# Decoding one f tile's weights ahead of the token forms, and storing the forms from other buffers

## The chip, the cores and the metric

The program runs on one core of a Trainium2 chip. The metric is the device time of one execution in microseconds, the median of several runs. The profile is of one further execution of the same program.

## The reference

Band attention (4 batches, 8 heads, 512 local and 32 global tokens, head size 64) gives 2176 tokens of 512 numbers. Two MLPs of the same size follow; each has 512 inputs, 2048 hidden units and 512 outputs:

```python
x = attention_out                      # 2176 x 512
h = x @ w_in                           # 512 -> 2048
g = np.where(h > 0, h, np.exp(np.minimum(h, 0)) - 1)
x = g @ w_out                          # 2048 -> 512
h = x @ w_in2
g = np.where(h >= 1, h, np.where(h <= -1, 0, (h + 1) ** 2 / 4))
out = g @ w_out2
```

Weights come as 64-bit floats and everything is done to more than single precision of one product: each factor is split into a high and a low part, and a product is three matmuls (low·high, high·low, high·high).

## The kernel before, in words

**Tiles.** The hidden units are cut into 16 f tiles of 128. Local tokens are cut into four blocks j of 512; the 128 global rows are a fifth block. `xh[j]`, `xl[j]` are the high and low parts of a token block, in two halves of [128, 2, 512]. An up product of one f tile and one block is 12 matmuls (L281), followed by the curve on ScalarE (L301, L303), the join on VectorE (L313), and the split into `gh` (ScalarE, L330) and `gl` (VectorE, L334). A down product is 12 matmuls into four PSUM banks (L368); at the end of a group of f tiles each bank goes through `collect`: ScalarE copies it to a tile `ev` (L347; four buffers), and a DMA stores it to DRAM (group of f tiles 0 to 2, from the SP queue, L350) or adds it there (later groups, an accumulating DMA from the GpSimd queue, L352).

**Stages of the first MLP.** `PLAIN = [[0, 1, 2], [3]]`: f tiles 0 to 3 are computed with plain products, 0 to 2 with weights that were decoded during the attention, f tile 3 with weights decoded behind it. f tiles 4 to 15, and the whole second MLP, are computed by pairs of f tiles with a Strassen-like scheme (`quad`, L1053): it needs seven "forms" of each duo of token blocks (X11, X21, X22 are halves of the blocks themselves; T2, T3, T1, T4 are sums and differences of them), each again in a high and a low part.

**Forms.** `first_forms(duo)` makes them for the first MLP: GpSimd adds high and low parts of four halves (L861: two into a tile `sum` of the pool `wraw`, two into the single buffers `top` and `rest`), VectorE makes four differences, and each of T2, T3, T1, T4 is split (`split`: ScalarE L951, VectorE L861) into a tile `form` and stored to DRAM (`keep`, two DMAs of 512 KB, L958). X11, X21 and X22 are stored from where they are. Before the first pair, T2, T3, T1 and T4 of duo 0 are loaded back (`load_form`, L1026) into the places of token blocks 2 and 3, once these have been used with f tile 3.

**Weights.** `words` loads raw 64-bit words (1 MB, L867) into a tile `wraw`; `decode` turns them into a high and a low part with two instructions on ScalarE (L213, L237) and seven on VectorE (L216 to L239), through the single buffers `top` and `rest`. `decode_one` does f tile 3 (into a tile tagged `wo0`). `decode_in(n)` does the first layer's side of pair n into a tile tagged `wi0`, `wi1` or `wi2` ([128, 2, 2048], 16 KB a partition), and then makes the Strassen sums of the weights on GpSimd (`whole`, `mixed`, L861), ScalarE (L909) and GpSimd again (`wi`). `decode_out(n)` does the second layer's side.

**Buffers.** The pool `wraw` has two buffers of 8 KB a partition. In the kernel before raw words, the tile `sum` and each tile `form` all go through it, in program order (`in_order("wraw", ...)`).

**Order.** The code issues work by events. An event is one up product or one part of a quad; after it one waiting group of down products is issued, and one or two background jobs go one step further. `job_at(n, job)` starts a job behind event n. Events 0 to 6 are the remaining up products of f tiles 0 to 2, event 7 the global rows, and then come the four up products of f tile 3. A scheduler then lays out each engine's queue: it follows that order, but puts an instruction that its model of times finds ready ahead of one that is not. On the chip each engine works its queue strictly in order.

Of the kernel before, what the change touches and what calls it, by code (L numbers as in the profile page):

```python
# [11 lines left out]
F32R = mybir.dt.float32r  # L12
# [9 lines left out]
B, H, SL, SG, D = 4, 8, 512, 32, 64  # L22
# [4 lines left out]
P = 128  # L27
# [13 lines left out]
PLAIN = [[0, 1, 2], [3]]  # L41
# [28 lines left out]
X11, X21, T2, T1, T3, T4, X22 = range(7)  # L70
# [7 lines left out]
def band_attention_then_two_mlps(  # L78
# [35 lines left out]
    def token_tile(j, h, part):  # L114

        return plain_p.tile([P, 2, SL], F32R, tag=f"x{part}{j}{h}", name="x" + "hl"[part])
# [59 lines left out]
    def in_order(tag, ins):  # L176


        if eng is free:
            if tag in newest:  # L180
                tc.add_manual_dep(ins.ins, newest[tag].ins.name, IN_ORDER, reason="order of tiles")
            newest[tag] = ins
# [241 lines left out]
    def mpool(name, bufs, **kw):  # L424
        return ctx.enter_context(tc.tile_pool(name=name, bufs=bufs, reuse_waits="tile", **kw))
# [424 lines left out]
    wraw_p = mpool("wraw", 2, side="right")  # L850
    wtmp_p = mpool("wtmp", 1, side="right")
    w_ps = [mpool("w_more", 1, side="right")]
# [6 lines left out]
    def add(out, a, b, op=ALU.add, engine=None):  # L859

        return (engine or eng.vector).tensor_tensor(out, a, b, op)  # L861

    def words(n, srcs):

        raw = wraw_p.tile([P, n * len(srcs)], U64, tag="wraw", name="wraw")
        for i, src in enumerate(srcs):
            ins = eng.sync.dma_start(raw[:, i * n:(i + 1) * n], src)  # L867
            if i == 0:
                in_order("wraw", ins)
        return raw  # L870

    def decode_one(f):

        w = w_ps[0].tile([P, 2, WCOLS], F32R, tag="wo0", name="wo")
        raw = words(WCOLS, [w1[f]])
        yield
        for _ in decode(wtmp_p, raw, w[:, 0], w[:, 1]):
            pass
        rows_in[0, 1] = lambda k, part: w[:, part, k * P:(k + 1) * P].rearrange("p (f c) -> p f c", f=1)
        w_in[0, f] = [w[:, i, 0:KT * P] for i in range(2)]  # L880
        w_out[0, f] = [w[:, i, KT * P:] for i in range(2)]

    def of_pair(n):

        layer, q = (0, n + 2) if n < 6 else (1, n - 6)
        return layer, (2 * q, 2 * q + 1)

    def decode_in(n):

        layer, fs = of_pair(n)  # L890
        raw = words(KT * P, [(w1, w2)[layer][f][:, 0:KT * P] for f in fs])
        yield
        w = w_ps[n % 3 // 2].tile([P, 2, 8 * BLOCK], F32R, tag=f"wi{n % 3}", name="wi")
        for _ in decode(wtmp_p, raw, w[:, 0, 0:4 * BLOCK], w[:, 1, 0:4 * BLOCK]):
            pass
        yield
        x = wtmp_p.tile([P, 4 * BLOCK], F32, tag="rest", name="whole")
        y = wtmp_p.tile([P, 4 * BLOCK], F32, tag="top", name="mixed")
        at = lambda t, c: t[:, c % (4 * BLOCK):c % (4 * BLOCK) + BLOCK]
        whole = add(  # L900
            x, w[:, 0, 0:4 * BLOCK].bitcast(F32), w[:, 1, 0:4 * BLOCK].bitcast(F32), engine=eng.gpsimd
        )
        in_order("rest", whole)
        in_order("top", add(at(y, S1), at(x, A21), at(x, A22), engine=eng.gpsimd))
        add(at(y, S2), at(y, S1), at(x, A11), ALU.subtract, eng.gpsimd)
        add(at(y, S3), at(x, A11), at(x, A21), ALU.subtract, eng.gpsimd)
        add(at(y, S4), at(x, A12), at(y, S2), ALU.subtract, eng.gpsimd)
        hi = w[:, 0, 4 * BLOCK:]
        eng.scalar.activation(hi, y, AF.Copy)  # L909
        add(w[:, 1, 4 * BLOCK:], y, hi.bitcast(F32), ALU.subtract, eng.gpsimd)  # L910
        pairs_in[n] = w
        rows_in[1, n] = lambda k, part: w[:, part, 0:4 * BLOCK].rearrange("p (f c) -> p f c", f=2)[
            :, :, k * P:(k + 1) * P
        ]

    def decode_out(n):

        layer, fs = of_pair(n)
        i = (n + 1) % 3
        raw = words(DM, [(w1, w2)[layer][f][:, KT * P:] for f in fs])  # L920
        yield

        while w_out_uses.get(n - 3):
            yield
        while len(w_ps) < 2:
            yield
        if i < 2:
            w = w_ps[i].tile([P, 2, 2, DM], F32R, tag=f"wo{i}", name="wo")
            w = [w[:, part] for part in range(2)]
        else:  # L930
            w = [token_tile(1, 0, part) for part in range(2)]
        for _ in decode(wtmp_p, raw, *(part.rearrange("p f d -> p (f d)") for part in w)):
            pass
        for i, f in enumerate(fs):
            w_out[layer, f] = [part[:, i] for part in w]
# [4 lines left out]
    def flat(t):  # L940

        return t.rearrange("p k n -> p (k n)")
# [6 lines left out]
    def split(out, src):  # L949

        ins = eng.scalar.activation(out[0], src, AF.Copy)  # L951
        add(out[1], src, out[0].bitcast(F32), ALU.subtract)
        return ins

    def keep(form, key, after=None):

        for part in range(2):
            ins = eng.sync.dma_start(forms[key][:, part], form[part].bitcast(F32))  # L958
            if after is not None:
                tc.add_manual_dep(ins.ins, after.ins.name, LANDED, reason="behind the loads")  # L960
        made_forms.add(key)

    def first_forms(duo):

        j0, j1 = 2 * duo, 2 * duo + 1
        s = wraw_p.tile([P, 2, 2 * SL], F32, tag="wraw", name="sum")
        x11, x21 = s[:, 0], s[:, 1]
        x12, x22 = (wtmp_p.tile([P, 2 * SL], F32, tag=tag, name="half") for tag in ("top", "rest"))
        for out, j, h, tag in ((x11, j0, 0, "wraw"), (x12, j1, 0, "top"), (x22, j1, 1, "rest"), (x21, j0, 1, "")):
            high, low = (flat(x[j][h]).bitcast(F32) for x in (xh, xl))  # L970
            ins = add(out, high, low, engine=eng.gpsimd)
            if tag:
                in_order(tag, ins)
        for i, j, h in ((X11, j0, 0), (X21, j0, 1), (X22, j1, 1)):
            keep([flat(x[j][h]) for x in (xh, xl)], (0, duo, i), last_low[0])
        yield
        add(x11, x12, x11, ALU.subtract)
        add(x12, x22, x12, ALU.subtract)
        add(x22, x22, x11, ALU.subtract)
        add(x21, x21, x22, ALU.subtract)  # L980
        for i, src in ((T2, x22), (T3, x12), (T1, x11), (T4, x21)):
            t = wraw_p.tile([P, 2, 2 * SL], F32R, tag="wraw", name="form")
            t = [t[:, part] for part in range(2)]
            in_order("wraw", split(t, src))
            keep(t, (0, duo, i))
            if i == T3:
                yield

    def later_forms(duo):
# [219 lines left out]
    def job_at(n, job, ahead=True):  # L1209

        due.setdefault(n, []).append((job, ahead))

    job_at(0, first_forms(0), False)
    job_at(2, first_forms(1), False)
    job_at(4, decode_one(PLAIN[1][0]))
    job_at(7, decode_in(0))
    job_at(9, decode_out(0))
    job_at(11, decode_in(1))
    for i, js in enumerate(((0, 1, 2, 3), (2, 3, 0, 1))):
        fs = PLAIN[i]  # L1220
        for j in js:
# [131 lines left out]
```

## Time and profile before

| | |
|---|---|
| runs | 891.52, 893.14, 897.77 us; median 893.14 us |
| profiled execution | 890.76 us, of which the span of the trace 889.0 us |
| mean granted TensorE clock | 0.975 of full speed |
| busy in the span | PE 818.1 us, VectorE 687.3 us, ScalarE 553.0 us, GpSimd 247.3 us |

PE is the matmul array, DVE VectorE, ACT ScalarE, POOL GpSimd, SP the SyncE queue that issues most DMAs. "L951" is line 951 of the kernel. Bracketed text behind an instruction is the idle time of its engine just before it, and what ended it. A DMA share is the mean busy share of the core's 16 DMA engines in a stretch; it can come out a little over 1.

### The profile page before, as it was taken

The page shows a single profiled execution, that of the slowest core. Times are in us where ns is not written, and L with a number is a line of the kernel's source. Part 1 is how long each engine was busy: PE and PEld are TensorE (multiplying, and loading weights), DVE is VectorE, ACT ScalarE, POOL GpSimd, SP SyncE. Part 2 cuts the span into 40 slices and gives each one's busy share as a digit, 9 for nine tenths or more (in the row PEclk, how much of TensorE's full clock was granted, in tenths as well). Part 3 has the DMA queues.
Part 4 walks back from the last instruction along what each step waited for, and adds up shares of the span by engine and source line. Part 5 has one row for each costly group of instructions (what it writes and reads, how often), then busy time and mean ns, then how long its engine had stood idle before and what let it go on. Part 6 is the DMA issues. An engine that isn't in the chain of part 4 may idle for free.

```text
span 889.0 us, 15955 instructions
## 1 busy us (share of the span) xinstructions
PE 818.1 (92%) x6058; PEld 663.3 (75%) x6058; DVE 687.3 (77%) x1187; ACT 553.0 (62%) x948; POOL 247.3 (28%) x254
## 2 busy tenths in 40 slices
PE   7899999906969999999999996999989999999998
PEld 5677778705757888888888875787878888888886
DVE  5888865518839799888797989999998699765464
ACT  5788846515636557665555537777776786777461
POOL 2222242203460724633240020214235143511000
PEclk9999999957989999999999999999999999999999
DMA  8978719577997738962972874725685398339723
GB/s 272 326 245 283 225 40 398 216 258 259 221 218 284 132 106 215 306 152 43 263 253 93 314 255 167 262 94 189 225 232 112 70 308 234 52 74 282 260 94 107
DMA packets 67132, 180.88 MB, mean 203 GB/s; under 512 B 9328, under 2 KB 9584, under 8 KB 65904
## 3 DMA queue, kind: packets, MB, share of 16 engines
q1 hardware_dynamic: 55248, 158.62, 51.1%
q0 software_dynamic: 11520, 20.98, 15.6%
q8 instruction: 48, 0.79, 0.4%
q10 hardware_dynamic: 288, 0.26, 0.1%
q14 instruction: 28, 0.23, 0.1%
HBM read 116.65 MB, written 63.18 MB: 202 GB/s over the span
## 4 chain that ended last, share of the span: by engine, by line
PE 54%; DVE 20%; issue 7%; ACT 6%; DMA 6%; POOL 6%; SPq 0%; ACTq 0%; POOLq 0%; DVEq 0%
PE dn L368 24%; PE up L1053 18%; DVE u L861 3%; DVE gl L334 2%; DVE g L315 2%; DMA sum<-ev 2%; PE up L281 2%; POOL mixed L861 2%; DVE rest L220 2%; POOL whole L861 2%; PE s L146 2%; PE dn L381 2%; DVE top L233 1%; POOL sum L352 1%; DMA wraw<-in_w 1%
## 5 line engine op out<-in xcount | busy, mean ns | idle before, releaser
L1053 PE MATMUL up<-xh,wi 128*128 128x512 f32 x784 | 263.2, 395 | 8.9 <-DVE u L861 6.0
L368 PE MATMUL dn<-gh,wo 128*128 128x512 f32 x608 | 189.3, 394 | 8.6 <-ACT ev L347 5.2
L1053 PEld LDWEIGHTS up<-xh,wi 128*128 128x128 f32 x784 | 148.7, 190 | 44.2 <-DVE u L861 9.4
L861 DVE TENSOR_TENSOR u<-up,u 128x512 f32<-128x512 f32 x196 | 130.6, 682 | 44.3 <-PE up L1053 26.5
L1053 PE MATMUL up<-xl,wi 128*128 128x512 f32 x392 | 154.2, 393 | 0.0
L368 PEld LDWEIGHTS dn<-gh,wo 128*128 128x128 f32 x608 | 113.1, 189 | 35.9 <-ACT ev L347 9.3
L330 ACT ACTIVATE gh<-g 128x512 fp32r<-128x512 f32 x123 | 77.2, 630 | 71.9 <-DVE g L315 35.4
L352 POOL DMA_DIRECT2D sum<-ev x80 | 75.3, 1167 | 160.9 <-ACT ev L347 160.0
L334 DVE TENSOR_TENSOR gl<-g,gh 128x512 fp32r<-128x512 f32 x123 | 101.8, 832 | 20.1 <-ACT gh L330 18.8
L368 PE MATMUL dn<-gl,wo 128*128 128x512 f32 x304 | 116.8, 391 | 0.3 <-DVE gl L334 0.3
L861 POOL TENSOR_TENSOR whole<-wi 128x1024 f32<-128x1024 f32 x14 | 36.7, 2619 | 257.8 <-DVE wi L239 246.7
L1053 PEld LDWEIGHTS up<-xl,wi 128*128 128x128 f32 x392 | 74.5, 190 | 15.1
L347 ACT ACTIVATE ev<-dn 128x512 f32<-128x512 f32 x110 | 61.3, 593 | 32.9 <-DMA sum<-ev 23.7
L315 DVE TENSOR_TENSOR g<-u,g 128x512 f32<-128x512 f32 x64 | 59.9, 940 | 27.8 <-ACT g L308 27.8
L306 ACT ACTIVATE g<-u,half_sb 128x512 f32<-128x512 f32 x64 | 46.0, 721 | 46.6 <-DVE u L861 40.0
L368 PEld LDWEIGHTS dn<-gl,wo 128*128 128x128 f32 x304 | 57.3, 189 | 12.9 <-DVE gl L334 0.7
L368 PE MATMUL dn<-gh,xl 128*128 128x512 f32 x160 | 62.5, 393 | 0.5 <-DVE xl L239 0.4
L368 PE MATMUL dn<-gh,xh 128*128 128x512 f32 x160 | 62.3, 390 | 0.0
L368 PE MATMUL dn<-gl,xh 128*128 128x512 f32 x160 | 59.2, 389 | 0.0
L301 ACT ACTIVATE g<-u 128x512 f32<-128x512 f32 x48 | 30.0, 627 | 42.3 <-DVE u L861 36.8
L307 ACT ACTIVATE g<-g,one_sb 128x512 f32<-128x512 f32 x68 | 48.6, 719 | 1.3
L313 DVE SCALAR_TENSOR_TENSOR g<-u,g 128x512 f32<-128x512 f32 x48 | 38.3, 803 | 13.3 <-ACT g L303 13.3
(189 smaller groups left out, 1488.5 us busy)
## 6 DMA issues: line engine op xcount, KB each, us to landing
wraw<-in_w SPq DMA_DIRECT2D x56, 512.0 KB, 6.1
xl<-form SPq DMA_DIRECT2D x46, 512.0 KB, 7.4
xh<-form SPq DMA_DIRECT2D x46, 512.0 KB, 9.0
sum<-ev POOLq DMA_DIRECT2D x80, 256.0 KB, 7.7
v_sb<-in_vwin SPq DMA_DIRECT2D x64, 260.0 KB, 4.9
form<-xh SPq DMA_DIRECT2D x20, 512.0 KB, 3.8
form<-xl SPq DMA_DIRECT2D x20, 512.0 KB, 4.0
sum<-ev SPq DMA_DIRECT2D x32, 256.0 KB, 3.1
```

Source lines behind the costliest of these rows:

```text
L301: eng.scalar.activation(self.g, self.ps, AF.Exp)
L306: eng.scalar.activation(self.g, self.ps, AF.Relu, bias=half_sb, scale=-0.5)
L307: eng.scalar.activation(self.g, self.g, AF.Relu, bias=one_sb, scale=-1.0)
L313: eng.vector.scalar_tensor_tensor(g, self.ps, 0.0, g, ALU.max, ALU.subtract)
L315: eng.vector.tensor_tensor(g, self.ps, g, ALU.max)
L330: eng.scalar.activation(self.gh, self.g, AF.Copy)
L334: eng.vector.tensor_tensor(self.gl, self.g, self.gh.bitcast(F32), ALU.subtract)
L347: eng.scalar.activation(out, ps, AF.Copy)
L352: eng.gpsimd.dma_start(to, out, accum_op=ALU.add)
L368: eng.tensor.matmul(banks[d], w[:, d * P:(d + 1) * P], g, start=first and k == 0, stop=last and k == 2)
L861: return (engine or eng.vector).tensor_tensor(out, a, b, op)
L1053: eng.tensor.matmul(ps, w[:, a, col + k * P:col + (k + 1) * P], x[b][:, k * SL:(k + 1) * SL], start=k + t == 0, stop=k == 1 and t == 2,)
```

## The change

Two things. The jobs start in another order: `decode_one` of f tile 3 at event 0, the forms of duo 0 at event 1 and of duo 1 at event 3 (before: forms at 0 and 2, `decode_one` at 4), and the first three jobs on pairs one or two events earlier. And the eight tiles `form` no longer come from the pool `wraw`: T2 and T3 of a duo go into one tile tagged `wi0`, T1 and T4 into one tile tagged `wi1`, the two single buffers that pairs 0 and 1 take later for their weights.

```diff
-        for i, src in ((T2, x22), (T3, x12), (T1, x11), (T4, x21)):
-            t = wraw_p.tile([P, 2, 2 * SL], F32R, tag="wraw", name="form")
-            t = [t[:, part] for part in range(2)]
-            in_order("wraw", split(t, src))
-            keep(t, (0, duo, i))
-            if i == T3:
+        for i, pair in enumerate((((T2, x22), (T3, x12)), ((T1, x11), (T4, x21)))):
+
+            t = w_ps[0].tile([P, 2, 2, 2 * SL], F32R, tag=f"wi{i}", name="form")
+            for k, (form, src) in enumerate(pair):
+                split([t[:, k, part] for part in range(2)], src)
+                keep([t[:, k, part] for part in range(2)], (0, duo, form))
+            if i == 0:
                 yield
...
-    job_at(0, first_forms(0), False)
-    job_at(2, first_forms(1), False)
-    job_at(4, decode_one(PLAIN[1][0]))
-    job_at(7, decode_in(0))
-    job_at(9, decode_out(0))
-    job_at(11, decode_in(1))
+    job_at(0, decode_one(PLAIN[1][0]))
+    job_at(1, first_forms(0), False)
+    job_at(3, first_forms(1), False)
+    job_at(5, decode_in(0))
+    job_at(8, decode_out(0))
+    job_at(10, decode_in(1))
```

## Rows read from the trace of the kernel before

**Rows 1.** The page, the span in 40 slices of 22.2 us: busy tenths, and granted TensorE clock.
```profile
PE   7899999906969999999999996999989999999998
PEclk9999999957989999999999999999999999999999
```
**Rows 2.** Waits of PE from 100 us on: waiter, releaser, total us, times, longest.
```profile
PE up L281 <- DVE wo L239: 30.6, 1, 30.6
PE up L1053 <- DVE u L861: 6.0, 5, 2.4
PE dn L368 <- ACT ev L347: 5.2, 5, 3.0
```
**Rows 3.** Chain of waits, 176 to 207 us: start, us, what.
```profile
181.34 1.06 ACT form L951
182.43 1.24 DVE form L861
183.68 2.64 DMA form<-form
186.42 1.06 ACT form L951
...
193.84 0.32 SPq L958
...
194.26 5.89 DMA wraw<-in_w
...
200.17 0.70 DVE rest L216
...
205.48 1.24 DVE wo L239
```
**Rows 4.** Timeline of PE around that wait: start, us, instruction.
```profile
175.81 0.39 PE L368 MATMUL dn<-gl,wh 128*128 128x512 f32 x1
206.76 0.79 PE L281 MATMUL up<-xh,wo 128*128 128x512 f32 x1 [30.56 <-DVE wo L239]
212.47 0.55 PE L281 MATMUL up<-xl,wo 128*128 128x512 f32 x1
226.72 0.40 PE L1053 MATMUL up<-xh,wi 128*128 128x512 f32 x1
```
**Rows 5.** Stretches of the span: length, busy us of each engine, granted clock, DMA share, GB/s.
```profile
110.00:120.00 10.00, 9.87 (x226) 7.68 (x218) 6.03 (x28) 6.20 (x14) 4.65 (x2) 1.00 0.02 5
130.00:175.80 45.80, 45.80 (x207) 38.17 (x206) 28.12 (x28) 25.48 (x40) 9.91 (x4) 1.00 0.77 297
175.80:206.76 30.96, 0.40 (x2) 0.00 (x1) 11.18 (x12) 7.52 (x9) 0.00 (x0) 0.55 0.62 229
206.76:240.00 33.24, 32.84 (x136) 26.38 (x136) 29.01 (x37) 20.64 (x35) 15.49 (x14) 0.91 0.94 269
240.00:260.00 20.00, 11.74 (x41) 8.37 (x41) 3.20 (x5) 6.48 (x11) 9.96 (x11) 0.91 1.06 250
```
**Rows 6.** Timeline of SP, DVE and POOL, around the end of the attention.
```profile
104.37 1.76 SPq L146 DMA_DIRECT2D v_sb<-in_vwin  x4
128.22 1.01 SPq L146 DMA_DIRECT2D sum<-ev  x2
145.19 1.18 SPq L958 DMA_DIRECT2D form<-xl  x1
115.35 4.73 POOL L861 TENSOR_TENSOR sum<-xh,xl 128x1024 f32<-128x1024 f32 x2 [7.25 <-PE s L146]
126.45 3.40 DVE L861 TENSOR_TENSOR sum<-half,sum 128x1024 f32<-128x1024 f32 x1 [1.34 <-POOL half L861]
124.03 4.75 POOL L861 TENSOR_TENSOR half<-xh,xl 128x1024 f32<-128x1024 f32 x2 [3.95 <-PE po L146]
```
**Rows 7.** Timeline of ACT and POOL: pair 0's weights into `wi`.
```profile
211.06 1.06 ACT L237 ACTIVATE wi<-top 128x1024 fp32r<-128x1024 f32 x1 [4.09 <-DVE top L233]
221.01 2.41 POOL L861 TENSOR_TENSOR wi<-mixed,wi 128x1024 fp32r<-128x1024 f32 x1 [1.97 <-ACT wi L909]
```

## The prediction

> **What bounds the kernel now.** I read first the strip of 40 slices on the page: PE is at nine tenths nearly everywhere, and the one slice that is empty is the ninth, 178 to 200 us, with the granted clock at about half in that slice and at 0.7 in the next [rows 1]. So PE bounds the kernel, and time lost by PE there is time of the kernel. Second, the waits of PE: one single wait of 30.6 us, the first up product of f tile 3 waiting for its decoded weights (`wo`, L239); no other group of waits from 100 us on is above 6.0 us in total [rows 2]. Third, what ended that wait, by the chain of waits: a store of a `form` lands, ScalarE and VectorE make the next one, it is stored, and so on, and behind the last of them the raw words of f tile 3 are loaded (5.89 us) and decoded [rows 3]. The forms are themselves not what PE waits for. They stand in its way only because raw words and forms share the two buffers of `wraw` and the program puts the raw words last. A form's work is 1.06 + 1.24 = 2.3 us, but one starts 5.1 us behind the other (181.34, 186.42), because each waits for the store of the one before to land [rows 3]. Fourth, the stretches: before the gap PE is busy all of 130 to 175.8 us; behind it there is a smaller hole, 8.3 idle us in 240 to 260 us, where the DMA share is 1.06 [rows 5] and in which PE waits for `ev` copies to empty its banks (5.2 us in all) [rows 2].
>
> **The decode of f tile 3 goes first.** Its load needs a `wraw` buffer; the first user of one in the trace starts at 115.35 us, released by the last scores of the attention [rows 6]. SP issues nothing between about 106 us and 128.22 us [rows 6] and the DMA share is 0.02 in 110 to 120 us [rows 5], so the load of 1 MB collides with nothing: 115.4 + 5.9 [rows 3] = 121.3 us. `top` and `rest` come free at 124.03 us (the add that waited for the attention's last product) [rows 6]. The decode itself runs from 200.17 to 205.48 + 1.24 = 206.72 us, 6.55 us [rows 3], so the weights are there at about 130.6 us. Even if other VectorE work spreads that over three times the time, they are there by 144 us, and PE wants them at 176. The gap is then gone: PE's last matmul before it starts at 175.81 us and takes 0.221 us (207 in 45.8 us [rows 5]), the next starts at 206.76 us [rows 4]: 206.76 − 176.03 = **30.7 us**. PE also restarts slow: 13 matmuls lie between 206.76 and 212.47 us [rows 4], 5.71 us instead of 13 × 0.221 = 2.9 us, with a granted clock of 0.55 in the gap [rows 5], which is the lower level (1.2 GHz) in nearly all of it. Without the gap that is another **2.8 us**. Sum: 33.5 us.
>
> **What is moved behind it: the forms.** The sums of duo 0 now wait for `top` and `rest` until 130.6 us instead of 124.03 us, 6.6 us later. I carry the rest of the chain from there: two adds on GpSimd 4.75 us [rows 6], four differences on VectorE, 3.40 us for the first, which ran beside GpSimd [rows 6], and three at 1.24 us, 7.1 us, four splits at 1.24 us [rows 3], 5.0 us. That is about 147 us for duo 0 and, the same 16.8 us again, 164 us for duo 1, with no round trip to DRAM in between; the last store lands 2.64 us later [rows 3], at 167. The other limit is DMA. A store of 512 KB takes 1.18 us of the queue when stores follow each other [rows 6]. There are 28 of them, 33 us; 16 stores of `ev` of half the size, 9.4 us; two loads of raw words for pair 0, four such units, 4.7 us. That is 47 us, which from 131.8 us, where the first stores of forms can start, ends at 179 us. I take the DMA limit, since the DMA share is 0.77 in that stretch already [rows 5]; the forms end between 167 and 179 us instead of about 196.5 us (193.84 + 2.64).
>
> **The added wait: `wi0` and `wi1`.** Pair 0's weights can be written only when T2 and T3 of duo 1 have been stored, pair 1's only after T1 and T4. By the DMA limit T2 and T3 have landed four stores before the end, at 179 − 4.7 = 174 us. From the first write into `wi` to the last add of GpSimd it took 211.06 to 223.42 us, 12.4 us [rows 7], so pair 0 is ready at about 187 us, or, with T2 and T3 landed at about 165 us by the other limit, at 177 us. PE wants it so long after the start of f tile 3 as before: 226.72 − 206.76 − 2.8 = 17.2 us of products at full clock [rows 4], that is at 193.2 us. The wait is hidden with about 6 us to spare; I cost it at nothing. The cover is f tile 3's own products. If it is not hidden, the instructions blocked are ScalarE's L237 and VectorE's L239, and behind them in their queues stand the curves, joins and splits of f tile 3 and the `ev` copies, so that PE stops for whatever the stores are late. Below nothing it cannot go, since nothing before used these buffers so early. The splits of duo 1 wait for duo 0's stores from the same tile in the same way; those were issued one duo's chain (some 17 us) earlier.
>
> **Queues.** The store count and load count are unchanged. On SP the load of f tile 3 moves ahead of all 28 stores, and 16 stores of T forms come closer together; the `ev` stores of f tiles 0 to 2 are issued between them and may land later. VectorE has 28.1 us of work in 130 to 175.8 us [rows 5]; the decode (6.5) and three more splits (3.7) make 38.3 of 45.8 us, and pair 0's decode comes to 44.8. It is the next engine to fill up. I charge nothing for that, and up to 5 us in the range: PE was at 100% there and an `ev` or a `gl` that comes late would show at once.
>
> **What is late next.** Once f tile 3 starts at 176 us, its 16 accumulating stores, the form loads and the next raw words come 31 us earlier with it. I take the hole of 240 to 260 us as it is, moved to about 209 to 229. The bounds are that it vanishes (8.3 us idle and some 2 us of clock more gained) or that it grows by what DMA has left over from the stores.
>
> **A rule that speaks against the change.** In 130 to 175.8 us the DMA engines are 0.77 busy, in 240 to 260 us 1.06 [rows 5]. The Trainium skill (DMA: Bandwidth & Descriptors, Issuing engines are not separate DMA queues) says that DMAs started by SP, ScalarE and GpSimd end on the same 16 engines and interleave. By that rule GpSimd's accumulating stores have no bandwidth of their own to escape into when SP's stores and loads are packed closer, and the gain would be the smaller one of the first rival below; the 1.06 agrees with it.
>
> **Rivals.** (a) DMA becomes the bound. From 130 to 260 us the shares times lengths add up to 0.77 × 45.8 + 0.62 × 31.0 + 0.94 × 33.2 + 1.06 × 20 = 107 us of full DMA [rows 5]; without the load that moves into the empty time, 104.5. If all of it had to be done before PE can go on and the engines kept 0.94, the best long stretch seen, it would end at 130 + 111 = 241 instead of 260 us: 19 us gained, 874 us. Against it: not all of it is on PE's path. (b) Pair 0 is late, because the forms are not made faster (ScalarE or VectorE too full, or the scheduler's order holds them up). If T3 of duo 1 lands at 183.68 + 2.64 = 186.3 us as before, pair 0 is there at 198.7, 5.5 us late, and with a slow restart 25 us are gained, 868 us; if it has to wait for the last store at 196.5 us, 209 us, 15.7 + 2.8 lost, 15 gained, 878 us. (c) The second hole shrinks too, because pair 1 and the raw words are ready earlier: 33.5 + 10 gained, 850 us. (d) Slower: the new wait on `wi0` holds ScalarE and VectorE in order so long that pair 0 is more than 33.5 us late, after 193.2 + 33.5 = 226.7 us. It decides from the point where T2 and T3 of duo 1 land after 226.7 − 12.4 = 214.3 us, 28 us later than before. At 5.1 us per round trip that needs more than five round trips more than the four it had, and with, say, eight it would be 13 us slower, 906 us. Nothing in the trace asks for that. (e) The change does not do what it says: the scheduler lays f tile 3's decode behind the forms on VectorE all the same, and the time stays within 1%, about 893 us.
>
> **How the numbers follow.** The profiled execution took 890.76 us; 890.76 − 33.5 = 857.3 us. The median of the runs is 2.4 us above that execution, so for a median I say 859.6, rounded to **860 us**. Chances: forecast (853 to 866) 0.54; (a) and (b), 866 to 880, together 0.24; (c), 846 to 853, 0.13; (e) 0.05; (d) 0.04. Faster by over 1% (8.9 us, about what the spread of the runs, 891.5 to 897.8, lets one tell) 0.91, within 1% 0.05, slower 0.04. The range takes in the forecast, (c) and (a): 848 to 874 us.
>
> **What would show it.** Right: no gap of PE between 170 and 210 us and a granted clock at full through it; the raw words of f tile 3 loaded near 116 us and decoded by 144 us; the forms' splits without a wait for DMA between them, ended by 180 us; the first pair's products (L1053) at about 193 us. Wrong: a wait of ScalarE L237 or VectorE L239 for `form` stores with PE idle behind it (b, d); PE waiting for `ev` in 180 to 230 us longer than the 8.3 us of before (a); PE idle before 176 us, where it had no idle time. The largest risk to the number is the second hole, which I only moved.

## The result and the profile after

The changed kernel takes 868.88 us (median of 4 runs, 867.27 to 870.86); the kernel before took 892.33 us on the same chip. The ratio is 0.9729, with an interval of 0.9678 to 0.9781: 23 us faster. A second set of runs of the same kernel, beside the experiments, gave 865.45 us and 0.9699 (0.9668 to 0.9730). So the gain is 23 to 27 us where 33.5 were forecast; the time is in the range of 848 to 874 us, the first median above the 853 to 866 us that the forecast itself was given.

The strip of 40 slices on the page of the changed kernel, a slice now 21.7 us, answers to [rows 1]:

```profile
PE   8899999998897999999999987999999999999998
PEclk9999999999898999999999999999999999999999
```

The empty slice is gone and the clock stays up where it had fallen to half. What is left, besides slices that were below nine before too, are eights and a seven between 195 and 282 us. The waits of PE from 100 us on (waiter, releaser, total us, times, longest) answer to [rows 2] (line 1054 is line 1053 of the kernel before; `u` is a partial result of a pair's products, on which VectorE adds up):

```profile
PE dn L368 <- ACT ev L347: 7.9, 5, 5.4
PE up L1054 <- DVE u L861: 6.4, 4, 2.4
PE up L1054 <- POOL wi L861: 3.2, 2, 2.6
PE up L281 <- DVE g L313: 3.0, 2, 2.0
...
PE up L1054 <- DVE wi L239: 3.0, 1, 3.0
```

The 30.6 us for `wo` do not occur any more. New are 3.0 us for joins of f tiles 0 to 2 (`g`, L313) and 3.0 us for pair 1's decode. The waits for `ev` did not grow. In the kernel before there is a second group of them, beside the 5.2 us of [rows 2], and the two make 8.8 us against the 7.9 us above:

```profile
PE dn L381 <- ACT ev L347: 3.6, 1, 3.6
```

The stretches (length, busy us and count of PE, PEld, DVE, ACT, POOL, granted clock, DMA share, GB/s) answer to [rows 5]:

```profile
130.00:175.80 45.80, 42.55 (x180) 34.31 (x180) 39.13 (x35) 26.43 (x39) 18.03 (x6) 0.96 0.84 324
175.80:206.76 30.96, 30.96 (x145) 25.50 (x144) 20.72 (x30) 19.36 (x34) 7.65 (x6) 1.00 1.00 362
206.76:240.00 33.24, 26.78 (x104) 20.85 (x104) 25.34 (x31) 19.16 (x31) 21.16 (x19) 0.85 0.89 225
240.00:260.00 20.00, 18.24 (x80) 14.46 (x79) 14.13 (x18) 9.64 (x15) 7.68 (x9) 1.00 1.07 289
```

The 31 us of the gap are now full. The stretch ahead of it is not: 180 matmuls where there had been 207 in 45.8 us [rows 5], with 3.25 idle us and the clock at 0.96, while VectorE went from 28.1 to 39.1 us and GpSimd from 9.9 to 18.0. The timeline shows the steps of the forecast and the two places where time was lost (start, us, instruction; lines of all engines, in order of time):

```profile
115.94 0.33 SPq L867 DMA_DIRECT2D wraw<-in_w  x1
131.34 1.23 DVE L239 SCALAR_TENSOR_TENSOR wo<-rest,wraw 128x1024 fp32r<-128x1024 uint32 x1
134.85 3.41 DVE L861 TENSOR_TENSOR sum<-half,sum 128x1024 f32<-128x1024 f32 x1 [2.29 <-POOL half L861]
137.14 6.74 POOL L861 TENSOR_TENSOR sum<-xh,xl 128x1024 f32<-128x1024 f32 x2
138.40 3.21 DVE L861 TENSOR_TENSOR half<-half 128x1024 f32<-128x1024 f32 x1
141.53 3.42 DVE L861 TENSOR_TENSOR form<-sum,form 128x1024 fp32r<-128x1024 f32 x1
148.28 0.68 DVE L313 SCALAR_TENSOR_TENSOR g<-up,g 128x512 f32<-128x512 f32 x1
149.02 0.79 PE L281 MATMUL up<-xh,wl 128*128 128x512 f32 x1 [2.01 <-DVE g L313]
161.08 1.22 DVE L861 TENSOR_TENSOR sum<-sum,half 128x1024 f32<-128x1024 f32 x1
170.65 1.99 ACT L951 ACTIVATE form<-half 128x1024 fp32r<-128x1024 f32 x2
176.21 1.22 DVE L861 TENSOR_TENSOR form<-sum,form 128x1024 fp32r<-128x1024 f32 x1
182.60 0.43 SPq L958 DMA_DIRECT2D form<-form  x1
192.42 2.40 POOL L861 TENSOR_TENSOR wi<-mixed,wi 128x1024 fp32r<-128x1024 f32 x1 [2.30 <-DMA sum<-ev]
194.60 0.45 PE L1054 MATMUL up<-xh,wi 128*128 128x512 f32 x1
214.84 0.79 PE L1054 MATMUL up<-xh,wi 128*128 128x512 f32 x1 [2.97 <-DVE wi L239]
254.85 22.72 SPq L867 DMA_DIRECT2D wraw<-in_w  x4
264.77 0.69 DVE L216 TENSOR_SCALAR rest<-wraw 128x1024 uint32<-128x1024 uint32 x1 [4.36 <-DMA wraw<-in_w]
266.10 0.60 ACT L301 ACTIVATE g<-up 128x512 f32<-128x512 f32 x1 [3.48 <-DVE gl L334]
267.24 1.22 PE L368 MATMUL dn<-gh,wo 128*128 128x512 f32 x2 [5.38 <-ACT ev L347]
```

Read downwards: the raw words of f tile 3 are requested at 115.94 us and decoded at 132.6. Then two differences and a split of duo 0 take VectorE 3.2 to 3.4 us each while GpSimd adds (to 143.88 us), the join at 148.28 us stands behind them, and PE waits for it. The last form is split at 177.4 us, its last store issued at 182.6, pair 0's weights are complete at 194.8 us, and the first pair's product starts at 194.60 us with no wait (its first products do not need the Strassen sums). The last hole is one queue behind another: a load of raw words, issued from 254.85 us on, is there only at 264.77 us (the DMA share is 1.03 to 1.07 in 250 to 265 us), VectorE's decode stands waiting for it (4.36 us), the split `gl` behind it comes late, so ScalarE's next curve (3.48 us), the `ev` copy behind that curve, and PE.

### The profile page after: what moved, and what is told of

Same layout as the page of the kernel before. It is cut to its first block, busy times and chain, and to the rows that moved or that the text cites. A ratio compares the mean times of both kernels' runs of the same rounds, so it can differ in the third digit from the quotient of the medians.

```text
span 869.1 us, 15955 instructions
## 1 busy us (share of the span) xinstructions
PE 823.2 (95%) x6058; PEld 668.8 (77%) x6058; DVE 684.4 (79%) x1187; ACT 552.8 (64%) x948; POOL 249.3 (29%) x254
## 4 chain that ended last, share of the span: by engine, by line
PE 54%; DVE 16%; issue 11%; DMA 9%; ACT 5%; POOL 4%; SPq 0%; DVEq 0%; POOLq 0%; ACTq 0%
PE dn L368 25%; PE up L1054 19%; DMA wraw<-in_w 5%; DMA sum<-ev 2%; DVE g L315 2%; DVE u L861 2%; PE s L146 2%; DVE gl L334 2%; PE dn L381 2%; DVE form L861 1%; POOL sum L352 1%; DVE rest L220 1%; PE up L146 1%; POOL mixed L861 1%; PE po L146 1%
## 5 line engine op out<-in xcount | busy, mean ns | idle before, releaser
L368 PEld LDWEIGHTS dn<-gh,wo 128*128 128x128 f32 x608 | 114.1, 189 | 35.8 <-ACT ev L347 10.2
L334 DVE TENSOR_TENSOR gl<-g,gh 128x512 fp32r<-128x512 f32 x123 | 97.0, 795 | 20.6 <-ACT gh L330 19.4
L1054 PEld LDWEIGHTS up<-xl,wi 128*128 128x128 f32 x392 | 74.5, 190 | 15.1
L315 DVE TENSOR_TENSOR g<-u,g 128x512 f32<-128x512 f32 x64 | 55.5, 869 | 26.6 <-ACT g L308 26.6
L313 DVE SCALAR_TENSOR_TENSOR g<-u,g 128x512 f32<-128x512 f32 x48 | 41.5, 869 | 19.2 <-ACT g L303 19.0
## 6 DMA issues: line engine op xcount, KB each, us to landing
xh<-form SPq DMA_DIRECT2D x46, 512.0 KB, 10.2
```

Source lines behind the costliest of these rows:

```text
L313: eng.vector.scalar_tensor_tensor(g, self.ps, 0.0, g, ALU.max, ALU.subtract)
L315: eng.vector.tensor_tensor(g, self.ps, g, ALU.max)
L334: eng.vector.tensor_tensor(self.gl, self.g, self.gh.bitcast(F32), ALU.subtract)
L368: eng.tensor.matmul(banks[d], w[:, d * P:(d + 1) * P], g, start=first and k == 0, stop=last and k == 2)
L1054: eng.tensor.matmul(ps, w[:, a, col + k * P:col + (k + 1) * P], x[b][:, k * SL:(k + 1) * SL], start=k + t == 0, stop=k == 1 and t == 2,)
```

## The experiments

Twelve runs in three sets, each set with its own runs of the kernel before (892.2 to 892.7 us). Ratios are to those, with 95% intervals.

**The order of jobs alone** (forms through `wraw` as before):

```diff
-    job_at(0, first_forms(0), False)
-    job_at(2, first_forms(1), False)
-    job_at(4, decode_one(PLAIN[1][0]))
...
+    job_at(0, decode_one(PLAIN[1][0]))
+    job_at(1, first_forms(0), False)
+    job_at(3, first_forms(1), False)
...
```

> The new order of jobs alone; the forms still go through the two buffers of wraw. Theory: the order fills the gap of PE at 176 to 207 us, but the forms keep their round trips to DRAM, and pair 0's raw words now stand behind them in the ring, so PE runs out of f tile 3's products near 195 us and waits for pair 0 until some 217 to 223 us: 880 to 889 us, most of the gain lost. Rival: only the place of f tile 3's decode matters; then this kernel is as fast as the whole change, 866 to 871 us.

893.39 us, 1.0014 (0.9988 to 1.0040): no gain at all, less than the theory gave. The stretches of this run:

```profile
130.00:200.00 70.00, 69.23 (x317) 57.28 (x315) 42.61 (x45) 41.38 (x67) 19.67 (x10) 1.00 0.86 306
200.00:230.00 30.00, 12.90 (x27) 7.33 (x27) 3.13 (x4) 9.52 (x16) 10.34 (x12) 0.53 1.08 228
230.00:270.00 40.00, 24.00 (x68) 16.91 (x69) 29.33 (x33) 14.50 (x18) 15.15 (x12) 0.71 0.50 155
```

and its timeline from the end of the forms on:

```profile
214.24 1.23 DVE L861 TENSOR_TENSOR form<-sum,form 128x1024 fp32r<-128x1024 f32 x1 [10.81 <-ACT form L951]
215.87 44.78 SPq L867 DMA_DIRECT2D wraw<-in_w  x10
228.14 1.22 PE L381 MATMUL dn<-wo,gh 128*128 128x512 f32 x2 [10.46 <-ACT ev L347]
229.61 0.69 DVE L216 TENSOR_SCALAR rest<-wraw 128x1024 uint32<-128x1024 uint32 x1 [14.14 <-DMA wraw<-in_w]
236.79 0.80 PE L1053 MATMUL up<-xh,wi 128*128 128x512 f32 x1 [7.01 <-DVE wi L239]
243.41 2.35 POOL L861 TENSOR_TENSOR wi<-mixed,wi 128x1024 fp32r<-128x1024 f32 x1 [1.17 <-ACT wi L909]
```

The gap at 176 us is filled: PE has 0.8 idle us in 130 to 200. It reappears behind f tile 3 in two waits: 10.46 us for `ev`, whose copies wait for f tile 3's accumulating stores, and 7.01 us for pair 0's weights, whose raw words now stand last in the ring. The forms end even later than before (215 instead of 194 us): the four round trips of duo 1 now run beside f tile 3's accumulating stores, at a DMA share of 1.08. The rival (only f tile 3's place matters) falls by 24 us.

**The buffers alone** (jobs in the old order):

> The new buffers of the forms alone, jobs in the old order. Theory: without the forms in the ring, f tile 3's raw words can be loaded once duo 0's sums are out of their buffer, and be decoded at about 165 to 178 us, about when PE wants them; the time is 865 to 875 us, near that of the whole change. Rival (the order is what matters): the decode still stands behind all the forms on ScalarE and VectorE and PE waits for it into the 180s or longer, 880 us or more.

862.88 us, 0.9660 (0.9624 to 0.9695): better than expected, and no worse than the whole change. PE's only wait for `wo` is the second line here (timeline of VectorE and PE):

```profile
137.57 3.42 DVE L861 TENSOR_TENSOR form<-half,form 128x1024 fp32r<-128x1024 f32 x1
173.77 0.80 PE L281 MATMUL up<-xh,wo 128*128 128x512 f32 x1 [4.42 <-DVE wo L239]
```

So f tile 3's decode comes out early enough, but for 4.4 us, in the old place too, once the forms are out of the ring. And PE loses nothing at 140 to 160 us here, although three of VectorE's instructions are stretched just as in the changed kernel (3.39, 3.42 and 3.41 us at 127.80, 137.57 and 142.05 us):

```profile
140.00:150.00 10.00, 10.00 (x46) 8.20 (x45) 10.00 (x9) 3.74 (x7) 3.31 (x1) 1.00 1.02 399
150.00:160.00 10.00, 10.00 (x47) 8.44 (x46) 7.77 (x11) 9.31 (x16) 0.00 (x0) 1.00 1.03 406
```

**The two duos' forms apart** (forms of duo 1 at event 5, pair jobs at 7, 9 and 11):

> The whole change, with the forms of duo 1 two events later (event 5) and the first three pair jobs at events 7, 9 and 11. Theory: the 5 us that PE loses at 140 to 162 us come from forms of both duos packed together on VectorE and from GpSimd's sums beside them, with the joins of f tiles 0 to 2 behind them in VectorE's queue; spread out, that loss falls by 3 us or more, and as pair 0 has a few us of cover the time is 863 to 867 us. Rival: pair 0 has no cover left, its weights come later by two events (some 10 us) and the time is 872 us or more.

865.52 us, 0.9697 (0.9661 to 0.9732), the same as the changed kernel within the intervals. The time lies in the expected span, but not for the expected reason: PE's idle time in 130 to 200 us is 3.19 us as before (table below), and GpSimd adds for 15.5 us in 130 to 150 as it did (15.1). So this edit didn't move what it was meant to move. That the scheduler starts the sums when their inputs are there, and not when the job is named, would explain it; it is not shown.

**f tile 3's results stored, not added.** This leaves out a sum of the reference. It also moves these 16 stores from the GpSimd queue to that of SP, so what it saves is the price of both together:

```diff
             to = sums[layer + 1, j][:, d, :]
-            if 0 in fs:
+            if fs == PLAIN[1]:
+                to = sums[0, j][:, d, :]
+            if 0 in fs or fs == PLAIN[1]:
                 eng.sync.dma_start(to, out)
```

in the changed kernel:

> The whole change, but the 16 results of f tile 3's down products are stored to a spare place in DRAM from the SP queue instead of being added to the sums (so the sum of f tiles 0 to 2 and of f tile 3 is not made; all else is done). Theory: what is missing of the forecast is lost because these accumulating stores, which come 31 us earlier now, keep the DMA engines and the ev buffers occupied between 205 and 270 us; without them the idle time of PE there (about 14 us) falls by half or more and the time is 858 to 864 us. Rival: pair 1's weights are late because VectorE decodes one weight after the other through single buffers; then nothing changes, 866 to 871 us.

and in the kernel before:

> The kernel before, with f tile 3's down products stored to a spare place instead of being added (so the sum with f tiles 0 to 2 is not made). Storing gained 13 us in the changed kernel. Theory: in the kernel before the accumulating stores cost less, the hole at 240 to 260 us with its slow clock, 8 to 11 us, so 882 to 885 us, and the difference of some 3 to 5 us is what the change lost by starting them earlier, beside other DMAs. Rival: they cost the same 13 us in both, 878 to 880 us; then nothing of the missing gain is theirs.

855.53 us, 0.9583 (0.9551 to 0.9616) in the changed kernel, which is 10 to 13 us less than with the accumulating stores; 883.81 us, 0.9911 (0.9882 to 0.9940) in the kernel before, 8 us less. The kernel before came out as its theory had it; the changed kernel is 2.5 us below the 858 to 864 us expected. PE's idle time in 200 to 300 us fell from 13.5 to 7.3 us in the one and from 17.0 to 12.7 in the other. Of what these stores cost the changed kernel, 8 us were there before. The 2 to 5 us more are not clear of the intervals, each of which is about 3 us wide to either side, so it is not shown that the stores cost more than before.

**Sums on VectorE:**

```diff
-            ins = add(out, high, low, engine=eng.gpsimd)
+            ins = add(out, high, low)
```

with the change, beside the unaltered changed kernel:

> The changed kernel unaltered, once more on the chip on which the next three run, so that they can be compared with it: 867 to 871 us.

> The change, with the eight sums of high and low parts on VectorE instead of GpSimd. Theory (sharing): five of VectorE's adds at 135 to 155 us take 2.8 to 3.4 us instead of 1.2 beside GpSimd, some 10 us, and the eight sums cost VectorE 8 x 1.23 = 9.9 us; the forms start earlier, since a sum takes 1.2 instead of 2.4 us, so the front loss falls by 1 to 3 us: 865 to 868 us. Rival: VectorE is so full that the sums only lengthen its queue: 870 us or more.

The unaltered kernel took 865.45 us; this one 854.23, 0.9578 (0.9547 to 0.9608), 11 us less, far outside the 1 to 3 us expected, and the fastest of all kernels here that leave nothing out. Its stretches, and below them those of the changed kernel:

```profile
130.00:140.00 10.00, 10.00 (x45) 8.26 (x45) 9.86 (x10) 4.58 (x7) 0.00 (x0) 1.00 1.03 393
140.00:150.00 10.00, 10.00 (x46) 8.27 (x45) 10.00 (x11) 6.03 (x10) 0.00 (x0) 1.00 1.02 411
150.00:160.00 10.00, 10.00 (x47) 8.40 (x46) 9.18 (x13) 8.77 (x16) 0.00 (x0) 1.00 1.01 356
```

```profile
140.00:150.00 10.00, 7.99 (x33) 6.28 (x33) 10.00 (x7) 6.09 (x8) 6.57 (x3) 0.95 1.03 404
150.00:160.00 10.00, 9.38 (x35) 6.95 (x33) 9.96 (x9) 2.99 (x5) 2.99 (x2) 0.88 0.99 371
```

VectorE is just as full, but does 11 and 13 instructions where it did 7 and 9, and PE never stops. Sums, the first difference and the first join in this run's timeline:

```profile
130.86 2.35 DVE L861 TENSOR_TENSOR half<-xh,xl 128x1024 f32<-128x1024 f32 x2
135.40 1.22 DVE L861 TENSOR_TENSOR sum<-half,sum 128x1024 f32<-128x1024 f32 x1
137.98 0.69 DVE L313 SCALAR_TENSOR_TENSOR g<-up,g 128x512 f32<-128x512 f32 x1
```

A sum costs VectorE 1.2 us and spares it about 2 us on the instruction that would have run beside GpSimd; over eight sums and five such instructions that is even, 9.8 us each way. What changes is when things come out: the first join behind the attention's end runs at 137.98 us instead of 148.28, and VectorE no longer waits for GpSimd's sums (2.29 us in the line at 134.85 us).

**Where the decode stands, and what the sums are worth elsewhere.** The decode between the two duos' forms (forms 0, decode 2, forms 3), with GpSimd's sums and with VectorE's; the old order with VectorE's sums; the kernel before with VectorE's sums; and pair 1's first-layer weights ahead of pair 0's second-layer weights, with VectorE's sums:

> The new buffers, and f tile 3's decode between the forms of duo 0 (event 0) and those of duo 1 (event 3) instead of ahead of both; pair jobs at 5, 8 and 10 as in the change. Theory: the 5 us that PE loses at 140 to 162 us come from the decode standing in front of duo 0's forms, which pushes their block on VectorE onto the joins of f tiles 0 to 2; the run with the buffers alone had no such loss but waited 4.4 us for its late decode. With the decode between, neither loss is there: 857 to 862 us. Rival: the block of forms costs PE the same wherever it lies, then 866 to 871 us.

> New buffers, sums on VectorE, and f tile 3's decode between the two duos' forms. Theory: PE loses nothing before 200 us in either place of the decode once the sums are on VectorE, so there is nothing left for the place to win: 852 to 857 us. Rival: the place is worth 5 us on its own, as with GpSimd's sums: 848 to 850 us.

> New buffers, old order of jobs, sums on VectorE. Theory: with the sums off GpSimd, the forms end earlier and leave VectorE's queue sooner, so the late decode of f tile 3 (PE waited 4.4 us for it with the buffers alone) is just in time or up to 4 us late: 853 to 859 us, the same as the new order with the sums on VectorE (854) or a little worse; so the new order alone would be worth 0 to 4 us, where with GpSimd's sums it cost some. Rival: the old order stays ahead by the same 3 to 5 us as with GpSimd's sums: 848 to 851 us.

> The kernel before with the eight sums on VectorE instead of GpSimd. Theory: what the sums cost the changed kernel (11 us) comes from forms packed against the joins of f tiles 0 to 2; in the kernel before the forms are held apart by their stores, PE loses nothing there, and the chain to f tile 3's weights gets shorter only by duo 1's two sums, 2 x 1.2, and the slow first difference, 2.2 us: 887 to 890 us. Rival: GpSimd's sums cost any kernel of this kind the same 11 us: 881 us.

> The change with sums on VectorE, and pair 1's first-layer weights started at event 8, pair 0's second-layer weights at event 10 (exchanged). With the sums on VectorE, PE still waits 2.9 us for pair 1's decode and some 4 us for ev buffers at 200 to 240 us. Theory: the decode's wait goes, the accumulating stores stay: 850 to 853 us. Rival: pair 0's down products now wait for their weights, and hold PE's queue: 856 us or more.

All runs, with PE's idle us and the count of matmuls from the stretches of each profile:

| kernel | us | ratio (interval) | idle 0-130 | idle 130-200 (matmuls) | idle 200-300 |
|---|---|---|---|---|---|
| before | 892 | 1 | 14.6 | 23.8 (208) | 17.0 |
| the change | 868.9 | 0.9729 (0.9678-0.9781) | 12.8 | 3.25 (294) | 13.6 |
| the change, second set | 865.5 | 0.9699 (0.9668-0.9730) | 11.2 | 3.2 (295) | 13.4 |
| order alone | 893.4 | 1.0014 (0.9988-1.0040) | 15.3 | 0.8 (317) | 33.6 |
| buffers alone | 862.9 | 0.9660 (0.9624-0.9695) | 13.7 | 4.4 (293) | 10.2 |
| forms apart | 865.5 | 0.9697 (0.9661-0.9732) | 12.4 | 3.2 (294) | 13.0 |
| change, stored | 855.5 | 0.9583 (0.9551-0.9616) | 13.8 | 4.5 (295) | 7.3 |
| before, stored | 883.8 | 0.9911 (0.9882-0.9940) | 13.2 | 22.6 (213) | 12.7 |
| decode between | 860.3 | 0.9634 (0.9605-0.9663) | 14.1 | 1.7 (311) | 11.7 |
| change, VectorE sums | 854.2 | 0.9578 (0.9547-0.9608) | 13.7 | 0.0 (320) | 9.8 |
| decode between, VectorE sums | 858.4 | 0.9629 (0.9598-0.9660) | 15.8 | 0.0 (320) | 9.7 |
| old order, VectorE sums | 862.7 | 0.9671 (0.9641-0.9700) | 16.5 | 2.6 (331) | 8.8 |
| pair 1 first, VectorE sums | 860.1 | 0.9645 (0.9604-0.9687) | 13.4 | 0.0 (320) | 14.9 |
| before, VectorE sums | 896.7 | 1.0057 (1.0030-1.0084) | 13.7 | 24.4 (205) | 21.1 |

The decode between is some 5 us better than the change, as its theory said (idle in 130 to 200 us 1.7 instead of 3.2 us, 16 matmuls further on). With VectorE's sums it is a little above the span expected, and not better than the change with them: PE loses nothing in 130 to 200 us in either, as expected, and its 4 us more do not lie in that stretch; 2.1 us of them are idle time in the first 130 us. The old order with VectorE's sums missed: 862.7 us instead of 853 to 859. Its early sums sit in VectorE's queue during the attention's last steps, where PE then waits 2.3 us for `xl` and the clock falls to 0.86 in 120 to 130 us. (Its 331 matmuls in the table take in small ones of the attention, which ends later there.) In the kernel before, VectorE's sums are 4 us slower, against both expectations: the chain to f tile 3 ends only 0.4 us earlier (f tile 3's first matmul at 206.37 us instead of 206.76 [rows 4]), since the stores set its pace, and the waits for `ev` behind it grow from 8.8 to 10.5 us. So the same edit, the sums on VectorE, is worth 11 us in the changed kernel, 2 with the decode between, nothing in the old order with the new buffers, and −4 us in the kernel before. The exchange of pair 1 and pair 0 ends in the rival's span, 6 us slower, but not by its mechanism: the wait for pair 1's decode shrinks as the theory had it (2.9 to 0.4 us), no down product waits for its weights, and PE waits 8.1 us for `ev` instead of 4.2 and 5.1 us for `wi` sums instead of 2.7.

## Why the prediction was right, and what it got wrong

**The gap: right in size.** What PE waited for was the ring, as read from the chain; the decode ended at 132.6 us (forecast 130.6), and 33.5 us of waiting and slow clock at 176 to 213 us are gone.

**Which edit does it: not as the steps put it.** The prediction booked the 33.5 us under the decode that goes first; of the new buffers it counted the earlier end of the forms as cover for pair 0, and an added wait that costs nothing. The runs with one edit each say the reverse: the order alone is worth 0 (−0.1 to +0.4%), the buffers alone 30 us. The order fills the gap and moves it behind f tile 3, for pair 0's raw words need the same ring. The step that the forms end by 179 us needed the buffers, and so does the whole gain. What the order adds to the buffers hangs on the sums: with GpSimd's it costs 3 to 6 us, within overlapping intervals; with VectorE's it gains 8 us (854.2 against 862.7 us).

**Forms and pair 0: later than forecast, but hidden.** The last store was issued at 182.6 us instead of landing at 179, pair 0 was complete at 194.8 instead of 187 us, and PE took its first pair's product at 194.6 (forecast 193). The wait on `wi0` stayed hidden. In the trace it is seen only as a pause: VectorE finished duo 1's last difference at 162.3 us, ScalarE's first split followed at 170.65, with the DMA share down at 0.53 in 160 to 170 us. That the scheduler laid the split so late on account of the buffer is argued, not shown.

**VectorE: mis-sized.** "I charge nothing for that, and up to 5 us in the range." It cost about 6 us: from 130 to 175.8 us PE did 180 matmuls of 0.221 us where the kernel before did 207, and at 200 us the changed kernel of the second set is 25 matmuls (5.5 us) behind its twin with VectorE's sums. PE idle before 176 us was one of the prediction's own signs of being wrong, and it came (3.25 us). That the engine of the sums makes this loss in this order of jobs is shown by that pair, since it is their only difference. Two effects are in it, and no run parts them: GpSimd's adds stretch five of VectorE's instructions to 2.8 to 3.4 us, with the joins queued behind them, and VectorE waits for adds that take GpSimd twice as long. Nor is a stretch a loss by itself: with the buffers alone three instructions were stretched and PE lost nothing there, and with the decode between PE waited for no join in 130 to 200 us (1.7 us idle, for `ev`). It became a loss with the decode ahead of both duos' forms. The row was there [rows 6]: its 3.40 us were put into the sum once, for one instruction, and the next ones were taken at 1.24. The Trainium skill (GPSIMD Engine Reference, Key points) says that GpSimd shares its SBUF interfaces with VectorE and contends with VectorE instructions that have two SBUF inputs; the rows agree, with 3.41 us for the first difference beside GpSimd's adds and 1.22 us for the same instruction without them.

**The second hole: mis-sized, and no longer the same hole.** It was moved "as it is", 8.3 us and some clock. PE idles 13.5 us in 200 to 300 us of the changed kernel against 10.2 us in the 93 us behind the gap in the kernel before (32.84 of 33.24 us, 11.74 of 20 and 38.43 of 40 busy in 206.76 to 300 us). But before, PE waited there for `ev`, 8.5 us in all. In the changed kernel it waits 2.97 us for pair 1's decode and 1.9 us for a `u`, then 5.38 us behind late raw words, and only 0.7 us for `ev` in 180 to 230 us. So the sign of rival (a), more than 8.3 us for `ev` in that stretch, did not come, and that the accumulating stores cost more than before is not shown. About half of the 11 us that VectorE's sums save lies behind 200 us (PE idle there 13.4 to 9.8 us, clock 0.95 to 0.97), so a part of this hole goes back to the packing ahead of it. How the rest is divided is not settled: each wait moves when the layout moves, and single executions of the changed kernel differ by up to 8 us.

33.5 less 5.5, less 3.3 for the added idle time, is 24.7 us; 23 to 27 were measured. The first median, 868.9 us, lies beside rival (b)'s 868 us, but that is luck: pair 0 was not late for PE. Rivals (d) and (e) did not occur, and (c), a second hole that shrinks, did not either.

## What to carry to other kernels

When a buffer ring serves several producers in program order, the wait is the ring's, not the last producer's: moving one user to the front only makes the next one last, and giving the bulky user buffers that lie idle frees all of them. Split such a change into its edits before you credit either; here one of the two was worth nothing by itself, and on top of the other it lost or gained with the engine of eight adds. And when work is packed closer on one engine, price each instruction at what it took beside the neighbour that it will now run beside, not at what it took alone, and ask what waits behind it in the queue.

## What the runs showed of the hardware

A two-input add, difference or split of 128x1024 on VectorE took 1.22 us alone and 2.80 to 3.42 us while GpSimd added. Two of GpSimd's adds of that size took 4.73 us [rows 6] and, beside VectorE's at 137.14 us, 6.74 us, so both can lose; one at 151.76 us took 2.39 us while the split beside it on VectorE took 3.03. Sixteen results of 256 KB added in DRAM from the GpSimd queue, instead of stored from that of SP, cost the kernel before 8 us and the changed kernel 10 to 13 us.
